# An attention-and-mixer kernel on one core: in what order a unit's products, the channel weights and GpSimd's sums are issued

## The chip, the core and the metric

The kernel runs on one core of a Trainium2 chip. A core has five engines that take their instructions in order, each from its own list: TensorE (PE in the profile, with its weight loads as PEld), VectorE (DVE), ScalarE (ACT), GpSimd (POOL) and SyncE (SP, which here only starts transfers). They wait for one another through semaphores. The metric is the device time of one execution in microseconds (us).

## The reference

Eight batches, eight heads of 64, sequence 576. First comes linear attention, then a mixer block of two small networks, one over the sequence and one over the channels:

```
q_s = softmax(q, over the head's 64);  k_s = softmax(k, over the 576 rows)
x   = q_s @ (k_s^T @ v)                         # per batch and head; heads side by side: x is 8 x 576 x 512
h   = relu(x^T @ w_tok1) @ w_tok2               # 576 -> 256 -> 576
u   = x + h^T
out = u + relu(u @ w_ch1) @ w_ch2               # 512 -> 1536 -> 512
```

The five activations are float32. The weights arrive as float64 and are turned into float32 in the kernel.

## The kernel before

**Work.** A unit is a batch b and a pair of heads j, 32 in all (n = 4b + j). The first eight (`NE`) are the early units, handled before the channel network begins; the others run between its steps. A group g is 512 columns of u, nine in all. A step (g, f) is one of twelve 128-wide slices of the 1536 channels: `ch1` forms 12 matmuls (L377) into a PSUM bank, ScalarE writes `h2h` = relu (L379) and VectorE the remainder `h2l` (L380); `ch2` forms 12 more (L388) into four accumulators `ps_o`. Every product of the channel network is done three times, high with high, high with low and low with high part, so weights and u exist as pairs (c1h/c1l, c2h/c2l, uh/ul). Emptying means taking a result out of PSUM: L379/L380 for a step, L365/L366 for a unit's u.

**A unit's stages.** `soft(n)` is both softmaxes (`softmax_k`: maximum L205, exponential L209, transposes L212 and L215 for an early unit; `softmax_q`: L233 to L239). `pe_stages(n)` gives four functions: the first transposes q and forms kv (`stage_qT` L282, for late units VectorE's transpose L294 and the copies L302; `stage_kv` L256, the reciprocal L262 and ScalarE's scaled copy `kvf`, L266), the second y (`stage_y`, L316, copied out in L318), the third h1 (`stage_h1`, L324, emptied in L331/L332) and the first half of u, the fourth the second half (`stage_u`, L359).

**Weights.** A piece is 128 x 512 float64 (512 KB). It is brought into a staging tile `stg` (L154, SyncE) and narrowed: VectorE L162, ScalarE L163, VectorE L164, L165, L167, L169. `split` (L102/L103) then makes the high part on ScalarE and the low one on VectorE. `load_tok1` brings w_tok1 in two pieces and a tail of half the width, `split_tok1` splits it for the late units, `load_tok2` brings w_tok2, and `load_ch(f)` two pieces, one of w_ch1 and one of w_ch2.

**Order.** The steps run (0, 0..3), (1, 0..11), (0, 4..11), then the groups 2 to 8. Early units are issued one after another, with unit n+2's loads and softmax ahead of unit n's h1 and u; `load_ch(0)` and `load_ch(1)` stand behind units 5 and 6, `load_ch(2)` to `load_ch(11)` before the steps 0 to 9. At the end of a group `residual` (GpSimd) forms uh + ul into a staging tile (L402). Group 0 is interrupted after four steps; its four accumulators are copied to `part` (L409), and after its last step GpSimd adds uh (L395) and ul (L396) to `part`. `out_end` adds the accumulators (L411, VectorE) and sends the result (L412, ScalarE's queue).

The text's order is a priority, not the final list: a scheduling pass places each instruction on its engine by readiness in a model of the time, earlier ones first. So an instruction that stands late in the text may run early, as L395 does. The list is fixed before the run.

```
        if n + 2 < NE:
            begin(n + 2)
            soft(n + 2)
        st[2]()
        st[3]()
```

Of the kernel before, what the change touches and what calls it, by code (L numbers as in the profile page):

```python
# [1 line left out]

# [6 lines left out]
F32 = mybir.dt.float32  # L9
F32R = mybir.dt.float32r  # L10
U32 = mybir.dt.uint32
AF = mybir.ActivationFunctionType
ALU = mybir.AluOpType
# [7 lines left out]
def attn_mixer_kernel(ctx: ExitStack, tc: tile.TileContext, q, k, kt, v, wt, out, dims):  # L21
# [15 lines left out]
    F_HEAD, F_MORE = 4, 8  # L37

    const = ctx.enter_context(tc.tile_pool(name="const", bufs=1))
    sm = ctx.enter_context(tc.tile_pool(name="sm", bufs=2))  # L40
    stg = ctx.enter_context(tc.tile_pool(name="stg", bufs=2))
    cv = ctx.enter_context(tc.tile_pool(name="cv", bufs=2))
# [24 lines left out]
    def kv_tile(pool, i):  # L67

        t = pool.tile([P, P], F32, name=f"kvf{i}")
        nc.gpsimd.memset(t, 0.0)  # L70
        return t
# [25 lines left out]
    def f32(ap):  # L97
        return ap.bitcast(F32)
# [87 lines left out]
    def split_tok1():  # L186
        split(w1h, w1l, w1f[:, 0:C, :], nc.vector)
        split(w1th, w1tl, w1t, nc.vector)
# [148 lines left out]
    uT = [slots[i] for i in (0, 1, 2, 1, 0, 2, 1, 0, 2)]  # L337
    assert len(uT) == NG

    def stage_u(u, half):  # L340
        b, j = u["b"], u["j"]
        edge = (b + 1) * CW - b * S
        cut = min(max(edge, S - 320), 320)
        n0, n1 = ((0, cut), (cut, S))[half]
        N = n1 - n0
        ns = slice(n0, n1)
        t = ps_unit()
        if u["early"]:
            mm = [(u["kvf"], u["qt"][:, ns])]
        else:  # L350
            mm = [(u["kvh"], u["qth"][:, ns]), (u["kvh"], u["qtl"][:, ns]), (u["kvl"], u["qth"][:, ns])]
        for n in range(NT):
            mm += [
                (u["hh"][:, n, :], w2h[:, n, ns]),
                (u["hh"][:, n, :], w2l[:, n, ns]),
                (u["hl"][:, n, :], w2h[:, n, ns]),
            ]
        for i, (a, w) in enumerate(mm):
            nc.tensor.matmul(t[:, 0:N], a, w, start=(i == 0), stop=(i == len(mm) - 1))  # L359
        for g, a0, a1 in ((b, n0, min(n1, edge)), (b + 1, max(n0, edge), n1)):  # L360
            if a0 < a1:
                at = b * S + a0 - g * CW
                uh, ul = (x[:, j, at : at + a1 - a0] for x in uT[g])
                src = t[:, a0 - n0 : a1 - n0]
                nc.scalar.copy(uh, src)  # L365
                nc.vector.tensor_tensor(ul, src, f32(uh), op=ALU.subtract)  # L366


    def ch1(g, f):
        hh = hpool.tile([P, CW], F32R, name="h2h")  # L370
        hl = hpool.tile([P, CW], F32R, name="h2l")
        t = ps_h.tile([P, 512], F32, name="ps_h")
        i = 0
        for n in range(NJ):
            uh, ul = (x[:, n, :] for x in uT[g])
            for a, w in ((c1h, uh), (c1l, uh), (c1h, ul)):
                nc.tensor.matmul(t, a[:, f, n, :], w, start=(i == 0), stop=(i == 3 * NJ - 1))  # L377
                i += 1
        nc.scalar.activation(hh, t, AF.Relu)  # L379
        nc.vector.scalar_tensor_tensor(hl, t, 0.0, f32(hh), op0=ALU.max, op1=ALU.subtract)  # L380
        return hh, hl

    def ch2(acc, f, first, last, hh, hl):
# [6 lines left out]
    def residual(g, n):  # L390

        uh, ul = (x[:, n, :] for x in uT[g])
        if g == 0:
            t = part[:, n, :]
            nc.gpsimd.tensor_tensor(t, t, f32(uh), op=ALU.add)  # L395
            nc.gpsimd.tensor_tensor(t, t, f32(ul), op=ALU.add)  # L396
            res[n] = t
            return
        if n % 2 == 0:
            t = stg.tile([P, CW, 2], U32, name="stg").rearrange("p n w -> p (n w)").bitcast(F32)  # L400
            res[n], res[n + 1] = t[:, 0:CW], t[:, CW : 2 * CW]
        nc.gpsimd.tensor_tensor(res[n], f32(uh), f32(ul), op=ALU.add)  # L402

    res = {}

    def out_end(g, acc, whole):
        for n, o in enumerate(acc):
# [9 lines left out]
    def begin(n):  # L417
        if n < NU and n not in units:
            units[n] = load_unit(n // NJ, n % NJ)

    def soft(n):
        if n < NU:
            softmax_k(units[n])
            softmax_q(units[n])
# [26 lines left out]
    w1t = early1.tile([P, TOK], F32, name="w1t")  # L451
    v_ring.append(v_tile(early1))
    kv_ring += [kv_tile(early1, i) for i in range(1, NB)]
    begin(0)
    load_v(0)
    soft(0)
    load_tok1()
    begin(1)
    load_v(1)
    soft(1)  # L460
    for n in range(NE):
        st = pe_stages(n)
        st[0]()
        st[1]()
        if n == 0:
            load_tok2()
        if n + 2 < NE:
            begin(n + 2)
            soft(n + 2)
        st[2]()  # L470
        st[3]()
        if n == NE - 4:
            split_tok1()
        if NE - 3 <= n < NE - 1:
            load_ch(n - (NE - 3))
    early_pools.close()
    del v_ring[1:], kv_ring[1:]
    ld = ctx.enter_context(tc.tile_pool(name="ld", bufs=2))
# [35 lines left out]
            put(x, fn)  # L514

    pend = None
    to_load = 2
    for i, (g, f) in enumerate(steps):
        if to_load < NF and (i < F_HEAD or g == 1):
            if to_load == F_MORE:  # L520
                more_pools.close()
                conv[:] = [(stg, cv)]
                c2_rows(F_MORE, NF)
            load_ch(to_load)
            to_load += 1
        h = ch1(g, f)
        for fn in todo.pop(i, []):
            fn()
# [73 lines left out]
```

## Time and profile before

| | |
|---|---|
| runs shown | 850.38, 851.43, 853.24 us; median 851.43 |
| the profiled execution | 851.01 us, its span (first to last instruction) 849.2 us |
| TensorE | 807.7 us busy (95%), 4464 matmuls, mean granted clock 0.995 |
| VectorE | 495.6 us (58%) |
| ScalarE | 323.8 us (38%) |
| GpSimd | 132.5 us (16%) |
| transfers | 63.54 MB, mean 75 GB/s |

How to read it: a line names engine, source line, operation, output tile <- input tiles and shape. In a group's line the numbers after the bar are busy time, mean ns of one, and the engine's idle time just before, with what ended it (`<-ACT h2h L379` is ScalarE's instruction of line 379 that writes h2h). A line of the timeline begins with start and duration in us; [1.42 <-DVE ...] is the idle time before it and its releaser. A line of waits gives total us, number of waits, longest. A busy TensorE is not TensorE at its peak, since matmuls are pipelined.

### The profile page before, as it was taken

Reading aid. Unit: us, or ns where it says so; the run is one execution under the profiler, and the core shown is the slowest. Engines: PE = TensorE matmul, PEld = TensorE weight load, DVE = VectorE, ACT = ScalarE, POOL = GpSimd, SP = SyncE. Lnnn points to the kernel's source line nnn. Section 1 sums busy time; section 2 is a strip of 40 time slices with the busy share of each in tenths; the row PEclk is TensorE's granted clock in tenths of the full one; section 3 lists DMA queues with packets and bytes.
Section 4 is the critical chain, followed back from the end, with each engine's and each line's share of the span. In section 5 each row is a group of like instructions: output and inputs, shape, how many; then the busy total and the mean of one; then the engine's idle time right before and its main releaser. Section 6 shows DMA issues by size and latency. Waiting matters only on the chain.

```text
span 849.2 us, 11727 instructions
## 1 busy us (share of the span) xinstructions
PE 807.7 (95%) x4464; PEld 671.8 (79%) x4464; DVE 495.6 (58%) x1076; ACT 323.8 (38%) x749; POOL 132.5 (16%) x104
## 2 busy tenths in 40 slices
PE   3779997998999999999999999999999999999997
PEld 2567885877888888888888888888888888888885
DVE  7899899988665555565557555755566322112111
ACT  4576552444553444344434344444344321011110
POOL 0000015042221111131113011311131102001000
PEclk9999999999999999999999999999999999999999
DMA  8543742223223222322213122312131001001001
GB/s 264 171 137 93 237 136 81 93 76 110 62 77 95 61 61 61 110 61 61 61 40 97 51 60 61 98 58 61 46 95 46 15 1 50 1 0 50 1 1 50
DMA packets 60632, 63.54 MB, mean 75 GB/s; under 512 B 40864, under 2 KB 40992, under 8 KB 60576
## 3 DMA queue, kind: packets, MB, share of 16 engines
q1 hardware_dynamic: 55392, 53.36, 21.5%
q10 hardware_dynamic: 5184, 9.44, 3.0%
q8 instruction: 35, 0.57, 0.3%
q14 instruction: 21, 0.17, 0.1%
HBM read 53.35 MB, written 9.44 MB: 74 GB/s over the span
## 4 chain that ended last, share of the span: by engine, by line
PE 76%; DVE 14%; DMA 5%; issue 2%; ACT 1%; POOL 1%; DVEq 0%; SPq 0%; POOLq 0%
PE ps_h L377 29%; PE ps_o L388 29%; PE ps_h L359 7%; PE ps_h L316 5%; PE ps_h L256 2%; DMA stg<-in_w 2%; DMA q_t<-in_q 2%; DVE q_t L302 2%; DVE stg L167 2%; DVE cv_s L169 1%; PE ps_h L324 1%; DVE cv_s L164 1%; DMA out<-stg 1%; PE ps_h L222 1%; DVE stg L165 1%
## 5 line engine op out<-in xcount | busy, mean ns | idle before, releaser
L380 DVE SCALAR_TENSOR_TENSOR h2l<-ps_h,h2h 128x512 fp32r<-128x512 f32 x108 | 74.0, 686 | 177.0 <-ACT h2h L379 177.0
L388 PE MATMUL ps_o<-h2h,c2h 128*128 128x512 f32 x432 | 169.9, 396 | 4.4 <-ACT h2h L379 4.4
L377 PE MATMUL ps_h<-uh,c1h 128*128 128x512 f32 x432 | 171.3, 396 | 0.0
L377 PE MATMUL ps_h<-ul,c1h 128*128 128x512 f32 x432 | 170.9, 396 | 0.0
L377 PE MATMUL ps_h<-uh,c1l 128*128 128x512 f32 x432 | 170.4, 394 | 0.0
L388 PE MATMUL ps_o<-h2h,c2l 128*128 128x512 f32 x432 | 169.8, 393 | 0.0
L379 ACT ACTIVATE h2h<-ps_h 128x512 fp32r<-128x512 f32 x108 | 64.3, 596 | 248.3 <-PE ps_h L377 240.7
L388 PE MATMUL ps_o<-h2l,c2h 128*128 128x512 f32 x432 | 154.6, 396 | 2.3 <-DVE h2l L380 2.3
L302 DVE COPY q_t<-cv_s 32x160 f32<-32x160 f32 (+1 forms) x264 | 72.8, 276 | 63.5 <-POOL ql L103 60.2
L388 PEld LDWEIGHTS ps_o<-h2h,c2h 128*128 128x128 f32 x432 | 81.7, 189 | 22.2 <-ACT h2h L379 5.3
L377 PEld LDWEIGHTS ps_h<-ul,c1h 128*128 128x128 f32 x432 | 81.3, 188 | 19.3
L388 PEld LDWEIGHTS ps_o<-h2l,c2h 128*128 128x128 f32 x432 | 79.6, 188 | 19.9 <-DVE h2l L380 3.6
L388 PEld LDWEIGHTS ps_o<-h2h,c2l 128*128 128x128 f32 x432 | 81.7, 189 | 16.8
L377 PEld LDWEIGHTS ps_h<-uh,c1h 128*128 128x128 f32 x432 | 81.3, 188 | 17.1
L377 PEld LDWEIGHTS ps_h<-uh,c1l 128*128 128x128 f32 x432 | 81.5, 189 | 16.8
L225 POOL TENSOR_TENSOR k_t<-k_t,mb 128x640 f32<-128x640 f32 x24 | 37.8, 1574 | 280.4 <-ACT mb L224 280.3
L402 POOL TENSOR_TENSOR stg<-uh,ul 128x512 f32<-128x512 f32 x32 | 41.6, 1324 | 155.8 <-DMA out<-stg 76.8
L103 POOL TENSOR_TENSOR ql<-q_t,qh 128x640 fp32r<-128x640 f32 x24 | 37.9, 1580 | 96.6 <-ACT qh L102 59.7
L233 DVE TENSOR_REDUCE st<-q_t 128x10 f32<-128x640 f32 x32 | 26.2, 818 | 42.5 <-DMA q_t<-in_q 42.5
L235 ACT ACTIVATE q_t<-q_t 128x640 f32<-128x640 f32 x32 | 23.6, 739 | 49.0 <-DVE q_t L234 49.0
L302 ACT COPY q_t<-cv_s 32x128 f32<-32x128 f32 (+1 forms) x120 | 36.8, 307 | 1.5
L359 PE MATMUL ps_h<-w2h,hh 128*128 128x256 f32 (+1 forms) x112 | 33.1, 303 | 1.4 <-ACT hh L331 1.4
(140 smaller groups left out, 1162.1 us busy)
## 6 DMA issues: line engine op xcount, KB each, us to landing
stg<-in_w SPq DMA_DIRECT2D x28, 512.0 KB, 3.7
kt_t<-in_kt SPq DMA_DIRECT2D x32, 320.0 KB, 3.5
q_t<-in_q SPq DMA_DIRECT2D x32, 320.0 KB, 3.0
v_t<-in_v SPq DMA_DIRECT2D x64, 128.0 KB, 3.0
out<-stg ACTq DMA_DIRECT2D x32, 256.0 KB, 2.7
k_t<-in_k SPq DMA_DIRECT2D x24, 320.0 KB, 3.6
v_t<-in_v SPq DMA_DIRECT2D x32, 32.0 KB, 3.1
out<-part ACTq DMA_DIRECT2D x4, 256.0 KB, 4.6
```

Of the source, the lines that this page charges most:

```text
L103: lo_eng.tensor_tensor(lo, src, f32(hi), op=ALU.subtract)
L225: nc.gpsimd.tensor_tensor(kx, kx, mb.unsqueeze(1).broadcast_to([P, C1, P]), op=ALU.subtract)
L233: nc.vector.tensor_reduce(st[:, 0, :], qt, axis=AX.X, op=ALU.max)
L235: nc.scalar.activation(qc, qc, AF.Exp)
L302: eng(qx[ys, 0:n, xs], turned[xs, 0:n, ys])
L316: nc.tensor.matmul(y[:, 0:TOK], a, w, start=(i == 0), stop=(i == len(mm) - 1))
L359: nc.tensor.matmul(t[:, 0:N], a, w, start=(i == 0), stop=(i == len(mm) - 1))
L377: nc.tensor.matmul(t, a[:, f, n, :], w, start=(i == 0), stop=(i == 3 * NJ - 1))
L379: nc.scalar.activation(hh, t, AF.Relu)
L380: nc.vector.scalar_tensor_tensor(hl, t, 0.0, f32(hh), op0=ALU.max, op1=ALU.subtract)
L388: nc.tensor.matmul(o, a[:, cs], w, start=(first and i == 0), stop=(last and i == 2))
L402: nc.gpsimd.tensor_tensor(res[n], f32(uh), f32(ul), op=ALU.add)
```

## The change

- An exponential on a one-column tile is issued first of all on ScalarE, after GpSimd has set the tile to zero.
- `load_tok1` stands ahead of unit 0's v, and unit 1's v and w_tok2 behind unit 1's softmax.
- Unit n+1's transposes, kv and y are issued ahead of unit n's h1 and u.
- `split_tok1` and the loads of f = 0 and 1 are wrapped in `behind(emptied)`, those from step 1 on in `behind(drained)`: each instruction that the block issues on ScalarE (on VectorE) is placed after the last emptying instruction on that engine. This orders instructions of one engine and adds no semaphore; the block's transfers, on SyncE, are not held.
- The loads stand before the steps 0, 1, 2, 3, 4, 6, 7, 9, 10, 12, where they stood before 0 to 9.
- Group 0's sums L395/L396 are placed behind the last residual of group 1 (L402).

```diff
     const = ctx.enter_context(tc.tile_pool(name="const", bufs=1))
+    warm = const.tile([P, 1], F32, name="warm")
+    nc.gpsimd.memset(warm, 0.0)
+    nc.scalar.activation(warm, warm, AF.Exp)
...
                 src = t[:, a0 - n0 : a1 - n0]
-                nc.scalar.copy(uh, src)
-                nc.vector.tensor_tensor(ul, src, f32(uh), op=ALU.subtract)
+                emptied[:] = [
+                    nc.scalar.copy(uh, src).ins,
+                    nc.vector.tensor_tensor(ul, src, f32(uh), op=ALU.subtract).ins,
+                ]
+    drained = []
+
+    @contextmanager
+    def behind(instructions):
+        with ExitStack() as stack:
+            for ins in instructions:
+                stack.enter_context(tc.issue_after(ins))
+            yield
...
-        nc.scalar.activation(hh, t, AF.Relu)
-        nc.vector.scalar_tensor_tensor(hl, t, 0.0, f32(hh), op0=ALU.max, op1=ALU.subtract)
+        drained[:] = [
+            nc.scalar.activation(hh, t, AF.Relu).ins,
+            nc.vector.scalar_tensor_tensor(hl, t, 0.0, f32(hh), op0=ALU.max, op1=ALU.subtract).ins,
+        ]
...
         if g == 0:
             t = part[:, n, :]
-            nc.gpsimd.tensor_tensor(t, t, f32(uh), op=ALU.add)
-            nc.gpsimd.tensor_tensor(t, t, f32(ul), op=ALU.add)
+            with behind(joined):
+                nc.gpsimd.tensor_tensor(t, t, f32(uh), op=ALU.add)
+                nc.gpsimd.tensor_tensor(t, t, f32(ul), op=ALU.add)
...
-        nc.gpsimd.tensor_tensor(res[n], f32(uh), f32(ul), op=ALU.add)
+        joined[:] = [nc.gpsimd.tensor_tensor(res[n], f32(uh), f32(ul), op=ALU.add).ins]
...
+    stages = [pe_stages(n) for n in range(NE)]
     begin(0)
-    load_v(0)
     soft(0)
     load_tok1()
+    load_v(0)
     begin(1)
+    stages[0][0]()
+    soft(1)
+    stages[0][1]()
     load_v(1)
-    soft(1)
+    load_tok2()
     for n in range(NE):
-        st = pe_stages(n)
-        st[0]()
-        st[1]()
-        if n == 0:
-            load_tok2()
         if n + 2 < NE:
             begin(n + 2)
             soft(n + 2)
-        st[2]()
-        st[3]()
-        if n == NE - 4:
-            split_tok1()
-        if NE - 3 <= n < NE - 1:
-            load_ch(n - (NE - 3))
+        if n + 1 < NE:
+            stages[n + 1][0]()
+            stages[n + 1][1]()
+        stages[n][2]()
+        stages[n][3]()
+        with behind(emptied):
+            if n == NE - 4:
+                split_tok1()
+            if NE - 3 <= n < NE - 1:
+                load_ch(n - (NE - 3))
...
-    to_load = 2
+
+    load_at = dict(zip((0, 1, 2, 3, 4, 6, 7, 9, 10, 12), range(2, NF)))
     for i, (g, f) in enumerate(steps):
-        if to_load < NF and (i < F_HEAD or g == 1):
-            if to_load == F_MORE:
+        if i in load_at:
+            if load_at[i] == F_MORE:
...
-            load_ch(to_load)
-            to_load += 1
+            with behind(drained):
+                load_ch(load_at[i])
         h = ch1(g, f)
```

More of the change, by code (lines that the diff above doesn't have):

```diff
@@ L1 @@
-from contextlib import ExitStack
+from contextlib import ExitStack, contextmanager
 import concourse.bass as bass
@@ L338, in attn_mixer_kernel @@
     assert len(uT) == NG
+    emptied = []
     def stage_u(u, half):
@@ L401, in residual @@
             res[n], res[n + 1] = t[:, 0:CW], t[:, CW : 2 * CW]
-        nc.gpsimd.tensor_tensor(res[n], f32(uh), f32(ul), op=ALU.add)
-    res = {}
+        joined[:] = [nc.gpsimd.tensor_tensor(res[n], f32(uh), f32(ul), op=ALU.add).ins]
+    res, joined = {}, []
     def out_end(g, acc, whole):
```

## The prediction

> **What bounds the kernel now.** I read the totals first, then the engines' busy times by stage, then who waits for whom on TensorE, then the order of time around its gaps.
>
> ```profile
> span 849.2 us, 11727 instructions
> PE 807.7 (95%) x4464; PEld 671.8 (79%) x4464; DVE 495.6 (58%) x1076; ACT 323.8 (38%) x749; POOL 132.5 (16%) x104
> ```
>
> ```profile
> 0.00:30.00 30.00, 13.17 (x80) 10.14 (x80) 24.71 (x56) 16.20 (x29) 2.12 (x16) 0.94 0.69 208
> 30.00:80.00 50.00, 41.68 (x317) 35.41 (x318) 44.87 (x110) 31.94 (x82) 0.00 (x0) 1.00 0.50 146
> 80.00:131.00 51.00, 51.00 (x259) 42.51 (x258) 48.41 (x91) 25.13 (x50) 7.43 (x5) 1.00 0.50 166
> 131.00:145.00 14.00, 8.75 (x32) 6.43 (x31) 14.00 (x18) 3.78 (x7) 7.70 (x5) 0.88 0.32 112
> 145.00:180.00 35.00, 35.00 (x171) 28.45 (x170) 33.95 (x56) 16.70 (x32) 7.96 (x6) 1.00 0.26 79
> 180.00:200.00 20.00, 15.89 (x78) 12.36 (x78) 16.17 (x40) 7.01 (x18) 2.90 (x2) 1.00 0.24 82
> 200.00:843.30 643.30, 642.21 (x3536) 536.49 (x3534) 311.67 (x710) 223.01 (x534) 104.38 (x72) 1.00 0.18 54
> ```
>
> The second fence's columns: stretch, its length, then the busy us (and number of instructions) of TensorE, weight load, VectorE, ScalarE, GpSimd, the granted clock, the transfers. TensorE is busy 807.7 of 849.2 us. The 41.5 idle us lie, window less busy: 16.8 before 30 us, 8.3 from 30 to 80, none to 131, 5.2 from 131 to 145, none to 180, 4.1 from 180 to 200, 1.1 to 843.3, and the last 5.9, in which only the output leaves. From 200 us on the matmuls run without a gap; the change keeps their number, so whatever it brings is TensorE idle time taken away, or added, before 200 us. No gain can pass the 34.5 us that are idle there, and the first gap is mostly waiting for the first data. The table's VectorE column is the second half of the picture: 24.7 of 30, 44.9 of 50, 48.4 of 51, 14 of 14, 34 of 35. In the head VectorE is nearly full, and its order decides who gets served.
>
> **The gaps of 30 to 80 us.** TensorE's waits in this window, all of them:
>
> ```profile
> PE ps_o L324 <- ACT kvf L266: 2.6, 2, 1.5
> PE ps_h L324 <- ACT kvf L266: 1.8, 2, 1.7
> PE ps_o L359 <- ACT hh L331: 1.7, 1, 1.7
> PE ps_o L324 <- ACT ys L318: 1.6, 1, 1.6
> PE ps_o L316 <- ACT qt L286: 0.8, 1, 0.8
> PE ps_h L256 <- DVE ul L366: 0.8, 1, 0.8
> ```
>
> They are a unit's chain: kv products, VectorE's reciprocal, ScalarE's scaled copy kvf, then h1 (L324). TensorE finds no product of the next unit in between.
>
> **The gap of 131 to 145 us.** In order of time, GpSimd's sums, VectorE beside them, TensorE and ScalarE behind:
>
> ```profile
> 123.57 5.23 POOL L395 TENSOR_TENSOR part<-part,uh 128x512 f32<-128x512 f32 x3 [120.72 <-ACT part L409]
> 133.57 5.13 POOL L396 TENSOR_TENSOR part<-part,ul 128x512 f32<-128x512 f32 x3
> ...
> 127.57 1.78 DVE L167 SCALAR_TENSOR_TENSOR stg<-stg 128x512 f32<-128x512 uint32 x1
> 129.27 3.21 DVE L165 TENSOR_SCALAR stg<-stg 128x512 uint32<-128x512 uint32 x2
> 132.41 0.68 DVE L380 SCALAR_TENSOR_TENSOR h2l<-ps_h,h2h 128x512 fp32r<-128x512 f32 x1
> ...
> 133.14 1.19 PE L388 MATMUL ps_o<-h2l,c2h 128*128 128x512 f32 x4 [1.42 <-DVE h2l L380]
> 140.94 0.80 PE L388 MATMUL ps_o<-h2h,c2h 128*128 128x512 f32 x1 [3.83 <-ACT h2h L379]
> ...
> 139.68 0.72 ACT L163 ACTIVATE cv_s<-cv_s,ebias 128x512 uint32<-128x512 uint32 x1 [4.49 <-DVE cv_s L162]
> ...
> 124.00:139.20 15.20, 15.20 (x12) 1.00 0.20 69
> ```
>
> The last line is VectorE alone in that stretch: full, with twelve instructions. While GpSimd adds, L167 takes 1.78 us and L165 1.6 each. The stretch up to 89.1 us gives the price without a sum:
>
> ```profile
> L167 DVE SCALAR_TENSOR_TENSOR stg<-stg 128x512 f32<-128x512 uint32 (+2 forms) x13 | 8.2, 627 | 0.0
> L164 DVE SCALAR_TENSOR_TENSOR cv_s<-stg,cv_s 128x512 uint32<-128x512 uint32 (+2 forms) x13 | 8.1, 626 | 0.0
> L169 DVE TENSOR_TENSOR cv_s<-stg,cv_s 128x512 f32<-128x512 f32 (+1 forms) x10 | 6.4, 637 | 0.0
> L162 DVE TENSOR_SCALAR cv_s<-stg 128x512 uint32<-128x512 uint32 (+2 forms) x14 | 5.5, 395 | 0.7 <-DMA stg<-in_w 0.7
> L165 DVE TENSOR_SCALAR stg<-stg 128x512 uint32<-128x512 uint32 (+2 forms) x13 | 5.1, 395 | 0.1
> L103 DVE TENSOR_TENSOR c1l<-cv_s,c1h 128x512 fp32r<-128x512 f32 x4 | 2.7, 679 | 0.0
> ```
>
> So VectorE loses 1.1 us on an L167 and 1.2 on an L165. Twelve instructions of 0.4 to 0.7 us are some 6 to 7 us of work, and they filled 15.2: about 9 us are lost. h2l (L380), which reads PSUM, is not longer (0.68). It comes late because it queues, and h2h because ScalarE sits before a weight piece's L163 that waits for VectorE's L162. TensorE loses 5.2 us, and 8.75 busy us at a granted clock of 0.88 cost 1.0 more: 6.3.
>
> **The change part by part.**
>
> ```profile
> 3.96 1.28 ACT L209 ACT_TABLE_LOAD   x1 [3.96 <-DMA kt_t<-in_kt]
> 20.23 1.21 DVE L103 TENSOR_TENSOR w1l<-w1f,w1h 128x1024 fp32r<-128x1024 f32 x1
> 27.16 0.42 DVE L169 TENSOR_TENSOR w1t<-stg,cv_s 128x256 f32<-128x256 f32 x1
> 28.30 0.60 PE L316 MATMUL ps_h<-w1f,q_t 128*128 128x256 f32 x2
> ```
>
> Early table load and a one-column memset: the load's 1.28 us move to before the first data. Unit 0's exponential follows it at once, but VectorE, which works on unit 0's q meanwhile, does not wait for it: I take 0, between 1.28 won and, were GpSimd's start late by the memset, the same lost.
>
> w_tok1 ahead of v on SP's queue, and its split late: the three transfers of unit 0's v are issued behind the three of w_tok1, and hidden as long as kv, which comes after the k softmax, is not early. Unit 0's y ends at 28.3 because the tail of w_tok1 is ready only at 27.2, with the split's w1l (1.21 us) ahead of it on VectorE. The split now stands behind unit 4's emptying, at the same price, where two channel pieces less stand. Gain 1.2 if only w1l leaves, 3 if y's whole wait moves up; loss 1 if v comes late. I take 1, nearest the lower bound, because the next limit is w_tok2, whose order to the units' softmax stays.
>
> A unit's first products ahead of the last unit's end: transposes, kv and y of unit n+1 now stand before h1 and u of unit n, so that the chain above has matmuls to hide behind: y alone is ten L316 of 0.3 us, by the row of two. What softmax and transposes of a unit ahead issue (SP's loads of kt and q too) keeps its place before them. The idle time is 8.3; between 0 and 8.3 I take 4.3, about what the two rows of kvf hold (4.4): the other four wait for ScalarE or VectorE themselves, which stay as full.
>
> ```profile
> 176.57 2.99 POOL L402 TENSOR_TENSOR stg<-uh,ul 128x512 f32<-128x512 f32 x2 [1.23 <-DVE cv_s L169]
> 178.33 5.08 DVE L302 COPY q_t<-cv_s 32x160 f32<-32x160 f32 x11
> 193.05 2.73 DVE L302 COPY q_t<-cv_s 32x160 f32<-32x160 f32 x11
> ```
>
> GpSimd's sums behind g=1's residuals (L402): 6.3 are won at 131 to 145. The eight sums run then after 176 us, where the last residuals of g=1 stand, into a stretch with VectorE busy 16.2 of 20. They are needed only at step 24, eight steps on, so GpSimd's own lateness costs nothing, but a late unit's softmax subtraction (L225) and ql can queue behind them, 1.7 us for each sum. The cost there is between 0 (they fall beside h2l alone) and the 9 that VectorE lost. I take 3: half of what it cost TensorE before, since no weight piece stands there any more.
>
> [...]
>
> Channel weights behind each step's emptying: no instruction and no semaphore is added, only order on VectorE and ScalarE; the loads on SP stay bound to their buffers, and softmax that was behind a held piece may go ahead of it. A piece costs 0.395+0.626+0.395+0.627+0.637+0.679 = 3.4 us of VectorE.
>
> ```profile
> 43.00:89.10 46.10, 39.99 (x314) 34.31 (x313) 42.71 (x106) 32.05 (x81) 0.00 (x0) 1.00 0.39 115
> 89.13 0.58 PE L377 MATMUL ps_h<-uh,c1h 128*128 128x512 f32 x1
> 174.12 1.77 DVE L103 TENSOR_TENSOR c1l<-cv_s,c1h 128x512 fp32r<-128x512 f32 x1
> ```
>
> Of the 13 L164 before 89.1 six are token weights, so seven channel pieces (23.6 us) were squeezed in between the units. Now two pieces wait for unit 5's emptying, two for unit 6's, two (step 0's load, whose list is still empty) for nothing, and the rest for steps. VectorE must still get through all of it: the last c1l ended at 175.9; less the 9 us of collision, 166.9, plus the time x that VectorE newly idles. TensorE wants it at: first product 89.1, less the 5.3 won above, 83.8; plus the old 86.9 from there to 176, less 6.3: 164.4. So it waits 2.5 + x. x is between 0 and the holes of the units' phase: 42.7 less 23.6 leaves 19.1 for units; with two to six pieces back (6.7 to 20.2) VectorE has 26 to 39 us of work beside TensorE's 40, so x is 1 to 14. I take x = 0 in the sum, near its lower end, since units that run closer together shorten the phase itself: a loss of 2.5.
>
> **Sum.** -1 - 4.3 - 6.3 + 3 + 2.5 = -6.1. The profiled execution took 851.0 (span 849.2 and 1.8 around it), 0.4 below the median of the runs, 851.43: 851.0 - 6.1 = 844.9.
>
> **Rivals.** A, both locks open: the head's chain waits vanish (-8.3), y moves up (-3), the sums cost nothing at their new place and the weights are never late: 851.0 - 8.3 - 3 - 6.3 = 833.4. For it speaks that TensorE ran 80 to 131 us with no idle while VectorE served everything; against it that VectorE has no slack until 180.
>
> C, the collision only moves: the sums block L302's copies and the late units' multiplications, and all 9 us reach TensorE, which already waits 4.1 us there: 844.9 + 6 = 850.9, no change. For it: the 5.08 beside 2.73. Against: TensorE has eight steps there that need only h2l.
>
> D, slower: the weights come too late. VectorE idles in the units' phase because pieces must stand behind emptyings, and the debt falls due at the last step of g=1. With x = 14 TensorE waits 16.5 instead of 2.5: 858.9. It decides from x = 8.7, where the time passes 851.0 + 2.6. For it: 48.4 of 51 and 34 of 35 busy us from 80 on leave nothing to catch up with. Against: step 0's unbound load, and 9 us of freed collisions.
>
> **How the numbers follow.** Forecast 0.50 (own range 838 to 849), A 0.15, C 0.15, D 0.20. About 0.3% (2.6 us) can be told from no change. The forecast gives faster but for 0.03, A faster, C 0.03 faster and the rest the same, D slower but for 0.01: faster 0.65, same 0.16, slower 0.19. The range 831 to 858 leaves out the far halves of A's and D's spread.
>
> **What would show it.** Right: L324's waits for kvf under 3 us before 80; L377's first product near 84; L395 behind L402, near 175; no gap over 2 us at 120 to 150; L165 at 0.4 there. Wrong: L377 waiting for c1h or c1l; VectorE idle between 45 and 80 by more than 8 us; L302's copies over 1 us each near 180 with h1 or u late; unit 0's kv waiting for v.

## The result: 14 us slower

The changed kernel took 865.19 us (median of five runs, 864.21 to 867.31); the kernel before took 850.38 beside it (850.14 to 853.24). The ratio is 1.0164, 95% interval [1.0143, 1.0185], that is 1.64% or 14.0 us; the two medians differ by 14.8. The prediction was 844.9, faster, and its range ended at 858.

Up to the first unit's stages the new lines are 3 further down than the old ones (L302 is now L305, L103 is L106, and what was L165 is now L168, while the new L165 is the old L162); the emptying of u is L371/L372, the first products of a step L393 (old L377), its emptying L396/L397, its second products L406 (old L388), GpSimd's sums into `part` L414/L415 (old L395/L396), its sums for the other groups L421 (old L402). First the totals of the page after:

```profile
span 865.5 us, 11729 instructions
...
PE 815.7 (94%) x4464; PEld 677.0 (78%) x4464; DVE 500.0 (58%) x1076; ACT 323.5 (37%) x750; POOL 128.6 (15%) x105
```

The span is 16.3 us longer (865.5 against 849.2; this execution, 867.31, is the longest of the five). TensorE is busy 8.0 us more with the same 4464 products, which is read below as a colder clock, about half of the loss; its idle time is 865.5 - 815.7 = 49.8 instead of 41.5, 8.3 more. The table by stage of the changed kernel, columns as in the prediction's second fence:

```profile
0.00:30.00 30.00, 14.16 (x78) 10.76 (x79) 23.40 (x52) 15.95 (x30) 2.15 (x17) 0.94 0.76 233
30.00:80.00 50.00, 50.00 (x383) 43.50 (x383) 37.34 (x97) 31.09 (x84) 0.00 (x0) 1.00 0.41 112
80.00:131.00 51.00, 37.85 (x144) 28.61 (x144) 46.01 (x89) 20.90 (x38) 1.82 (x1) 0.87 0.46 155
131.00:145.00 14.00, 14.00 (x62) 11.45 (x62) 14.00 (x27) 8.12 (x15) 0.00 (x0) 1.00 0.34 112
145.00:180.00 35.00, 35.00 (x155) 28.57 (x154) 31.64 (x56) 14.26 (x25) 3.54 (x3) 1.00 0.35 115
180.00:200.00 20.00, 9.79 (x67) 7.82 (x66) 19.83 (x22) 3.92 (x11) 15.26 (x12) 0.85 0.13 32
200.00:220.00 20.00, 18.41 (x95) 14.50 (x96) 16.05 (x35) 9.36 (x25) 3.75 (x3) 0.90 0.31 104
```

What was to go is gone: TensorE's idle 8.3 us of 30 to 80, and 5.2 of 131 to 145. What came: 13.2 us idle at 80 to 131, where there were none; 10.2 at 180 to 200, where there were 4.1; and 1.6 behind it. The clock column carries the rest: 37.85 busy us at 0.87, 9.79 at 0.85 and 18.41 at 0.90 lose 4.9 + 1.5 + 1.8 = 8.2, where the kernel before lost 1.0 at 131 to 145. Now the VectorE column: between 30 and 80 it is busy 37.3 of 50, where it was 44.9. The engine that was nearly full now stands still for 12.7 us, while TensorE does not wait at all.

TensorE's waits to 300 us in the changed kernel (total, number, longest), the four of them that stand for the two new gaps:

```profile
PE ps_o L406 <- DVE h2l L397: 11.5, 2, 10.2
PE ps_h L393 <- ACT c1h L105: 7.2, 3, 5.2
...
PE ps_o L406 <- ACT h2h L396: 3.5, 4, 1.9
...
PE ps_h L393 <- DVE c1l L106: 1.4, 1, 1.4
```

And its timeline, read from three engines: SyncE's weight transfers (start, duration), VectorE's work on the weights (L165 begins a piece, L172 is the last to read its staging tile, L106 forms its low part) and TensorE's wait for it, then GpSimd's sums with VectorE and TensorE beside them (the row of eleven copies holds six of 32x160 and five of 32x128):

```profile
35.48 0.33 SPq L157 DMA_DIRECT2D stg<-in_w  x1
41.45 0.34 SPq L157 DMA_DIRECT2D stg<-in_w  x1
81.11 0.34 SPq L157 DMA_DIRECT2D stg<-in_w  x1
...
75.44 0.75 DVE L165 TENSOR_SCALAR cv_s<-stg 128x512 uint32<-128x512 uint32 x2
80.41 1.28 DVE L172 TENSOR_TENSOR cv_s<-stg,cv_s 128x512 f32<-128x512 f32 x2
82.21 0.68 DVE L106 TENSOR_TENSOR c1l<-cv_s,c1h 128x512 fp32r<-128x512 f32 x1
98.11 0.63 DVE L106 TENSOR_TENSOR c1l<-cv_s,c1h 128x512 fp32r<-128x512 f32 x1
...
96.64 0.80 PE L393 MATMUL ps_h<-uh,c1h 128*128 128x512 f32 x1 [5.24 <-ACT c1h L105]
...
183.96 2.55 POOL L421 TENSOR_TENSOR stg<-uh,ul 128x512 f32<-128x512 f32 x2 [2.56 <-DVE cv_s L172]
186.46 5.00 POOL L414 TENSOR_TENSOR part<-part,uh 128x512 f32<-128x512 f32 x4
191.41 1.54 POOL L228 TENSOR_TENSOR k_t<-k_t,mb 128x640 f32<-128x640 f32 x1
192.89 4.93 POOL L415 TENSOR_TENSOR part<-part,ul 128x512 f32<-128x512 f32 x4
...
183.81 12.88 DVE L305 COPY q_t<-cv_s 32x160 f32<-32x160 f32 x11
199.12 0.65 DVE L397 SCALAR_TENSOR_TENSOR h2l<-ps_h,h2h 128x512 fp32r<-128x512 f32 x1
...
199.82 0.80 PE L406 MATMUL ps_o<-h2l,c2h 128*128 128x512 f32 x1 [10.21 <-DVE h2l L397]
```

By 41.45 ten weight transfers have been issued, six pieces of token weights and the four of f = 0 and f = 1, which fill the four staging tiles. The pieces of f = 0 wait for unit 5's emptying and begin at 75.44 (L165). The next transfer, the first piece of f = 2, goes out only at 81.11: until 68.96 SyncE's list holds other loads, and then it waits 12.1 us for VectorE's L172, the last reader of a held staging tile. The low part c1l of f = 0 is formed at 82.2, just in time, that of f = 1 only at 98.1, and TensorE waits. At the other gap eleven short copies take 12.88 us beside GpSimd's sums, and h2l, which TensorE needs, is behind them in VectorE's list.

### The profile page after: what moved, and what is told of

It is laid out like the page before. It is cut to its first block, busy times and chain, and to the rows that moved or that the text cites. A ratio compares the mean times of both kernels' runs of the same rounds, so it can differ in the third digit from the quotient of the medians.

```text
span 865.5 us, 11729 instructions
## 1 busy us (share of the span) xinstructions
PE 815.7 (94%) x4464; PEld 677.0 (78%) x4464; DVE 500.0 (58%) x1076; ACT 323.5 (37%) x750; POOL 128.6 (15%) x105
## 4 chain that ended last, share of the span: by engine, by line
PE 72%; DVE 16%; DMA 7%; issue 2%; ACT 1%; POOL 1%; SPq 0%; DVEq 0%; POOLq 0%; ACTq 0%
PE ps_h L393 26%; PE ps_o L406 26%; PE ps_h L364 7%; PE ps_h L319 5%; DMA stg<-in_w 4%; DVE q_t L305 3%; PE ps_h L259 2%; DMA out<-stg 2%; DVE cv_s L172 1%; DMA q_t<-in_q 1%; DVE cv_s L167 1%; PE ps_o L364 1%; PE ps_h L327 1%; DVE stg L170 1%; DVE h2l L397 1%
## 5 line engine op out<-in xcount | busy, mean ns | idle before, releaser
L393 PE MATMUL ps_h<-uh,c1h 128*128 128x512 f32 x432 | 172.8, 400 | 7.2 <-ACT c1h L105 7.2
L397 DVE SCALAR_TENSOR_TENSOR h2l<-ps_h,h2h 128x512 fp32r<-128x512 f32 x108 | 74.1, 687 | 176.7 <-ACT h2h L396 176.4
L406 PE MATMUL ps_o<-h2h,c2h 128*128 128x512 f32 x432 | 171.6, 398 | 3.5 <-ACT h2h L396 3.5
L393 PE MATMUL ps_h<-uh,c1l 128*128 128x512 f32 x432 | 171.7, 398 | 1.4 <-DVE c1l L106 1.4
L393 PE MATMUL ps_h<-ul,c1h 128*128 128x512 f32 x432 | 171.8, 398 | 0.0
L406 PE MATMUL ps_o<-h2h,c2l 128*128 128x512 f32 x432 | 170.7, 395 | 0.0
L406 PE MATMUL ps_o<-h2l,c2h 128*128 128x512 f32 x432 | 155.4, 399 | 11.5 <-DVE h2l L397 11.5
L396 ACT ACTIVATE h2h<-ps_h 128x512 fp32r<-128x512 f32 x108 | 64.2, 595 | 241.0 <-PE ps_h L393 236.0
L305 DVE COPY q_t<-cv_s 32x160 f32<-32x160 f32 (+1 forms) x264 | 80.6, 305 | 64.0 <-POOL ql L106 60.8
L406 PEld LDWEIGHTS ps_o<-h2l,c2h 128*128 128x128 f32 x432 | 80.4, 190 | 29.0 <-DVE h2l L397 12.4
L393 PEld LDWEIGHTS ps_h<-uh,c1h 128*128 128x128 f32 x432 | 82.1, 190 | 25.6 <-ACT c1h L105 8.4
L406 PEld LDWEIGHTS ps_o<-h2h,c2h 128*128 128x128 f32 x432 | 82.1, 190 | 22.0 <-ACT h2h L396 4.9
L393 PEld LDWEIGHTS ps_h<-uh,c1l 128*128 128x128 f32 x432 | 82.2, 190 | 19.1 <-DVE c1l L106 2.0
L393 PEld LDWEIGHTS ps_h<-ul,c1h 128*128 128x128 f32 x432 | 82.0, 190 | 19.4
L406 PEld LDWEIGHTS ps_o<-h2h,c2l 128*128 128x128 f32 x432 | 82.0, 190 | 16.9
L228 POOL TENSOR_TENSOR k_t<-k_t,mb 128x640 f32<-128x640 f32 x24 | 38.0, 1582 | 321.6 <-ACT mb L227 321.6
L106 POOL TENSOR_TENSOR ql<-q_t,qh 128x640 fp32r<-128x640 f32 x24 | 37.8, 1576 | 194.2 <-ACT qh L105 158.7
L421 POOL TENSOR_TENSOR stg<-uh,ul 128x512 f32<-128x512 f32 x32 | 41.2, 1308 | 158.3 <-DMA out<-stg 82.7
L305 ACT COPY q_t<-cv_s 32x128 f32<-32x128 f32 (+1 forms) x120 | 36.8, 307 | 6.1 <-DVE cv_s L297 4.5
```

The costliest lines, as they stand in the source:

```text
L106: lo_eng.tensor_tensor(lo, src, f32(hi), op=ALU.subtract)
L228: nc.gpsimd.tensor_tensor(kx, kx, mb.unsqueeze(1).broadcast_to([P, C1, P]), op=ALU.subtract)
L305: eng(qx[ys, 0:n, xs], turned[xs, 0:n, ys])
L396: nc.scalar.activation(hh, t, AF.Relu).ins,
L406: nc.tensor.matmul(o, a[:, cs], w, start=(first and i == 0), stop=(last and i == 2))
L421: joined[:] = [nc.gpsimd.tensor_tensor(res[n], f32(uh), f32(ul), op=ALU.add).ins]
```

## The experiments

All in one table. Each ratio is against the kernel before in the same set of runs. "None held" is the changed kernel without the holds on channel weights.

| | us | ratio to before, 95% |
|---|---|---|
| changed kernel | 865.19 | 1.0164 [1.0143, 1.0185] |
| none held (`a_nohold`) | 841.18 | 0.9868 [0.9836, 0.9901] |
| units' pairs held, steps' free (`a_holdunits`) | 857.02 | 1.0042 [1.0023, 1.0061] |
| steps' held, units' pairs free (`a_holdsteps`) | 848.61 | 0.9951 [0.9934, 0.9968] |
| only f = 0 held (`n_hold0`) | 858.27 | 1.0066 [1.0040, 1.0092] |
| only f = 1 held (`n_hold1`) | 859.28 | 1.0077 [1.0053, 1.0101] |
| f = 0 held, more scratch (`n_hold0scr`) | 859.44 | 1.0091 [1.0074, 1.0108] |
| none held, units in the old order (`n_oldunits`) | 851.87 | 0.9980 [0.9959, 1.0002] |
| none held, old start (`n_oldstart`) | 853.03 | 0.9998 [0.9985, 1.0012] |
| none held, w_tok1's split free (`n_splitfree`) | 842.62 | 0.9883 [0.9847, 0.9918] |
| none held, old steps of the loads (`n_oldload`) | 841.15 | 0.9863 [0.9840, 0.9886] |
| before with the units' new order (`b_units`) | 850.86 | 0.9969 [0.9948, 0.9991] |
| changed, units in the old order (`a_oldunits`) | 860.44 | 1.0118 [1.0088, 1.0147] |
| before with late sums (`b_sumslate`) | 853.73 | 1.0022 [1.0002, 1.0042] |
| changed with free sums (`a_sumsfree`) | 869.59 | 1.0199 [1.0173, 1.0225] |
| before without sums (`b_nosums`) | 844.28 | 0.9897 [0.9867, 0.9927] |
| changed without sums (`a_nosums`) | 861.14 | 1.0092 [1.0066, 1.0119] |
| none held, without sums (`n_nosums`) | 839.79 | 0.9832 [0.9799, 0.9865] |
| none held, sums on TensorE (`n_sumspe`) | 837.46 | 0.9811 [0.9786, 0.9836] |

### The holds on channel weights

First everything that is held on `load_ch` was let go; w_tok1's split stays held.

```
-            with behind(drained):
-                load_ch(load_at[i])
+            load_ch(load_at[i])
...
-            if NE - 3 <= n < NE - 1:
-                load_ch(n - (NE - 3))
+        if NE - 3 <= n < NE - 1:
+            load_ch(n - (NE - 3))
```

> The changed kernel with the loads of channel weights no longer ordered behind emptyings (w_tok1's split still is, and the spread-out places of the loads stay). Theory W, the held weights starve TensorE: the 13.2 us idle between 80 and 131 us fall under 3, with most of the cold clock there (about 5 us at 0.87), the gap at 180 to 200 stays near 10: about 850 us, 15 less than the changed kernel. Rival V, VectorE has simply too much work before the last weight: the idle time only moves to 30 to 80 us or to 140 to 180, and the time stays within 3 us of 865.

It took 841.18: the loss turned into a gain, and the holds cost 1.0164 - 0.9868 = 2.96%, 25 us. Its table by stage, and SyncE's transfers:

```profile
30.00:80.00 50.00, 49.63 (x386) 43.52 (x385) 48.19 (x122) 36.21 (x93) 0.00 (x0) 1.00 0.53 142
80.00:131.00 51.00, 51.00 (x230) 41.87 (x229) 48.90 (x95) 25.18 (x46) 2.19 (x1) 1.00 0.51 167
...
180.00:200.00 20.00, 16.73 (x95) 13.60 (x95) 17.54 (x31) 7.95 (x22) 12.01 (x9) 0.91 0.36 109
...
49.70 0.34 SPq L157 DMA_DIRECT2D stg<-in_w  x1
67.43 15.51 SPq L157 DMA_DIRECT2D stg<-in_w  x5
```

VectorE is full again between 30 and 80 (48.2), transfers go out at 49.7 and from 67.4 on, and the gap of 80 to 131 is gone. Then each half of the holds by itself:

```
 a_holdunits:  of the diff above, only load_ch(load_at[i]) is let go
 a_holdsteps:  only load_ch(n - (NE - 3)) is let go
```

> The changed kernel with only the two channel pairs behind units 5's and 6's emptyings held; the pieces loaded in the steps are free. What is open: which of the two holds costs the 24 us between the changed kernel (865) and the one without either (841). Theory Wu (the held pieces of the units' phase sit in the four staging tiles, so that the next transfer cannot be issued before they go, and VectorE stands idle 12.7 us between 30 and 80): this kernel is as slow as the changed one, 858 to 868, with TensorE waiting for c1h or c1l near 96 and VectorE busy 36 to 39 in 30 to 80. Rival Ws (the holds behind the steps keep the late pieces back): most of the 24 us are won here, 840 to 848, VectorE busy over 44 in 30 to 80, no gap at 80 to 131.

> The mirror: the changed kernel with only the pieces loaded in the steps held behind each step's emptying; the pairs of units 5 and 6 are free. Theory Wu: nearly all is won, 840 to 848, TensorE idle under 2 us in 30 to 131, VectorE busy over 44 in 30 to 80. Rival Ws: 855 to 866, with TensorE waiting for c1h or c1l in the steps.

Both halves cost. The units' pairs cost 2.13% (18 us) with the steps' held and 1.74% (15 us) with them free; the steps' cost 1.22% (10 us) and 0.83% (7 us). The first theory holds for the larger part, its rival for the smaller; both times lie about 1 us outside the ranges that the first theory had given. The kernel with the units' pairs held, then the one with the steps' held:

```profile
30.00:80.00 50.00, 49.50 (x383) 43.07 (x382) 37.76 (x99) 31.09 (x84) 0.00 (x0) 1.00 0.39 107
80.00:131.00 51.00, 37.00 (x137) 27.43 (x136) 47.27 (x90) 21.77 (x39) 1.80 (x1) 0.83 0.50 165
```

```profile
30.00:80.00 50.00, 48.99 (x382) 42.91 (x381) 48.12 (x120) 35.28 (x92) 0.00 (x0) 1.00 0.50 142
80.00:131.00 51.00, 45.95 (x200) 37.27 (x199) 46.42 (x89) 23.58 (x43) 1.68 (x1) 0.93 0.48 155
```

It is the units' holds that empty VectorE's list between 30 and 80; 14 idle us of TensorE follow behind 80. With the steps' held alone VectorE stays full, and 5 us follow. Which piece of the units' phase does it?

```
-        if NE - 3 <= n < NE - 1:
-            load_ch(n - (NE - 3))
+            if n == NE - 3:              # behind(emptied); n_hold1: n == NE - 2
+                load_ch(0)               #                  n_hold1: load_ch(1)
+        if n == NE - 2:                  # free;            n_hold1: n == NE - 3
+            load_ch(1)                   #                  n_hold1: load_ch(0)
```

> The version without holds on channel weights (841.2), with only the pair of f = 0 held behind unit 5's emptying; the pair of f = 1 and all the rest are free. With both pairs held it took 857.0. Theory R (the held pieces sit in the rings of staging and scratch tiles, whose later users wait: it is the first held piece that stops VectorE's supply, and f = 1 and f = 2 queue behind it): most of the 16 us are here, 850 to 857, VectorE busy 37 to 43 in 30 to 80. Rival E (what costs is the late piece itself, f = 1, which TensorE waited 5.2 us for at 96): 841 to 846, VectorE busy over 45.

> The mirror: only the pair of f = 1 held, behind unit 6's emptying; f = 0 is free. Theory R: f = 0 passes through and only the supply behind f = 1 stops, for less time: 843 to 850, VectorE busy 42 to 46 in 30 to 80. Rival E: 850 to 857, with TensorE waiting some 5 us for c1h of f = 1 near 96.

Each pair alone costs 17 us (1.98% and 2.09% above none held), as much as both. So neither theory was right: not the first held piece alone, and not one late piece. Either hold is enough. VectorE was busy 37.8 of 50 in the one and 38.6 in the other, and f = 1 was late in both, also where it was not held itself. In the kernel with f = 0 alone held, the c1l of f = 0 and f = 1:

```profile
81.87 0.68 DVE L106 TENSOR_TENSOR c1l<-cv_s,c1h 128x512 fp32r<-128x512 f32 x1
...
98.09 0.63 DVE L106 TENSOR_TENSOR c1l<-cv_s,c1h 128x512 fp32r<-128x512 f32 x1
```

How does the hold reach f = 1 where f = 1 is free? It uses the two scratch tiles that f = 0 uses, and two more were added:

```
+    cv_early = early_pools.enter_context(tc.tile_pool(name="cv_early", bufs=2))
-    conv[:] = [(stg, cv), (stg_more, cv)]
+    conv[:] = [(stg, cv), (stg_more, cv_early)]
```

> The version with only f = 0's pair held (858.3), with two scratch tiles more in the units' phase, so that the free pair of f = 1 no longer waits for the scratch tiles of the held one; the staging tiles stay four. Theory R (the rings pass a hold on to the pieces behind it): f = 1's c1l, at 98.1 in the version with two scratch tiles, comes before 92, TensorE's wait of 5.6 us for c1h near 96 is gone, 848 to 854. Rival Q (the order of VectorE's list alone, in which a late piece stands behind the late units' softmax, whatever tiles are free): 856 to 860, c1l of f = 1 still after 95.

```profile
87.75 0.68 DVE L106 TENSOR_TENSOR c1l<-cv_s,c1h 128x512 fp32r<-128x512 f32 x1
...
93.80 0.68 DVE L106 TENSOR_TENSOR c1l<-cv_s,c1h 128x512 fp32r<-128x512 f32 x1
```

f = 1 came 4 us earlier, not the 6 that were expected, and f = 0 came later. The time was no better (859.44, in the range of rival Q, whose date for f = 1 it missed): VectorE was busy 34.3 us between 30 and 80, and the next weight transfer after that of 32.2 went out at 85.7. So the scratch tiles alone are not the way. VectorE's timeline of this kernel (L373 is the emptying of u, L166 the first instruction of a piece) shows what is:

```profile
78.17 0.29 DVE L373 TENSOR_TENSOR ul<-ps_h,uh 128x128 fp32r<-128x128 f32 x1 [0.26 <-ACT uh L372]
78.38 1.43 DVE L166 TENSOR_SCALAR cv_s<-stg 128x512 uint32<-128x512 uint32 x4
```

The four are the pieces of f = 0 and f = 1. Those of f = 1 are not held, had been issued to their staging tiles by 33.8 and had scratch tiles of their own; still they run in one row with the held ones. What kept them is their place in VectorE's list, which is fixed before the run. The transfers behind them wait for the staging tiles: 12.1 us of queue time in the changed kernel, 13.8 here. In every kernel with a held pair VectorE idles 11 to 16 us between 30 and 80, in those of the new order without one 1.2 to 1.9.

### The unit order, the start and the split

```
 b_units: before, with the loop of the change
     for n in range(NE):
         begin(n + 2); soft(n + 2)
+        stages[n + 1][0](); stages[n + 1][1]()
         stages[n][2](); stages[n][3]()
```

> The kernel before with one part of the change: a unit's transposes, kv and y ahead of the last unit's h1 and u; weights, sums and start as before. Theory U, the order of products alone fills TensorE's gaps: idle in 30 to 80 us falls from 8.3 to under 3, about 844 us. Rival V, VectorE is full there, so that the gaps only come back elsewhere before 200 us: 849 to 852.

It took 850.86, 0.3% [0.1%, 0.5%] below before, and TensorE's idle time in 30 to 80 was 8.5 as ever. Its longest wait there, of the list of waits, then TensorE and VectorE on the timeline:

```profile
PE ps_o L282 <- issue: 7.4, 1, 7.4
...
48.90 1.09 PE L282 MATMUL ps_o<-ident,q_t 128*128 128x128 f32 x4 [7.35 <-issue]
...
48.03 0.78 DVE L239 TENSOR_TENSOR q_t<-q_t,st 128x640 f32<-128x640 f32 x1
```

The waits for kvf are gone, and one wait of the same size has come: the transposes of the next q now stand ahead in TensorE's list, and that q's last softmax step (L239) ends on VectorE at 48.8. The profile names no releaser for this wait; the step that ends 0.1 us ahead is read as its cause. With none held, the unit order and the start were put back one at a time, and the split was freed:

```
 n_oldunits:  none held, loop of before (stages 0 to 3 of unit n in one turn); with it
              load_v(1) ahead of soft(1) again, stages[0][0:2] behind it
 n_oldstart:  none held, load_v(0), load_v(1) and soft(1) ahead again, stages[0][0:2] behind them
 n_splitfree: none held, split_tok1() not held either
```

> The version without the holds on channel weights (841.2), with the units' loop in the order of before: a unit's first products stand behind the last unit's end again; the start order, w_tok1's late split and the sums' new place stay. What is open: the unit order alone on the kernel before moved nothing (850.9, TensorE idle 8.5 in 30 to 80), yet the version without holds has 0.4 there. Theory H (the order of units needs the earlier start: only with both are there ready products to hide behind): the idle time of 30 to 80 comes back to 6 to 9 us, total 847 to 850. Rival H2 (the gap closes because loads and VectorE are earlier by the start order, whatever the units' order): under 2 us idle there, total 840 to 843.

> The version without holds (841.2), with the start in the order of before (v of units 0 and 1 ahead, unit 0's transposes and y behind unit 1's softmax); units' order, late split and the sums' place stay. The unit order was worth 10.7 us on this version and 1.5 to 3 on the kernel before. Theory H (it needs the earlier start: with the old one a transposed q put ahead waits for VectorE): 847 to 851, with TensorE idle 4 to 8 us in 30 to 80. Rival K (it needs w_tok1's late split or the sums' place, not the start): 841 to 844, under 2 us idle there.

> The version without the holds on channel weights (841.2), and w_tok1's split also bound to nothing, so that VectorE may take it as soon as w_tok1 is loaded, as before. Theory L (the late split is what starts the units early: 1.3 to 1.8 us of VectorE in the first 30 us, and less before each unit's q): TensorE's idle time before 30 us rises by 1 to 1.5 from 15.6, 842 to 844. Rival L2 (the split fits into a hole of VectorE's in the head): within 0.8 us of 841.2.

With none held, `n_oldunits` costs 1.1% (9.5 us) and `n_oldstart` 1.3% (11 us), both more than theory H had; the unit order alone, on the kernel before, had won 0.3%. TensorE's idle time in 30 to 80 is 8.5 with the new unit order alone, 6.9 in `n_oldstart`, 7.7 in `n_oldunits` and 0.4 with both. So the first products of a unit hide the chain of the last one only if the unit ahead has been made ready earlier: with the old start the same wait as above came back (4.3 us at 47). The converse is not shown. `n_oldunits` takes back a part of the start too (unit 0's first products stand behind unit 1's softmax in it and in `n_oldstart`), and no kernel has the whole new start with the old order. Nor is all of the 11 us the start's: in `n_oldstart` a late unit's eleven copies fell beside the sums (12.87 us at 170.8), and TensorE waited 10.5 us for h2l behind them. The late split's share is 0.15%, inside the interval.

> The version without holds (841.2), with the channel weights of f = 2 to 11 loaded in steps 0 to 9, one in each, as before, where the change spreads the last five over steps 6, 7, 9, 10 and 12. Nobody's theory gave this part a price: if it only shifts what VectorE does in its full stretch, 840 to 843; if the spread is what keeps weight pieces out of the way of the late units, 844 to 848.

(`load_at` is again 0 to 9.) 841.15, as with the new steps: this part moves nothing. Last, the old unit order in the changed kernel itself, with its holds:

> The changed kernel (865.2) with the units' loop in the order of before; the holds and the rest stay. The unit order was worth 10.7 us where nothing was held. Theory H (it closes the gaps of 30 to 80, and what is won there is lost again where TensorE waits for held weights): 864 to 868, with 6 to 9 us idle in 30 to 80 and less idle time in 80 to 131. Rival G (its worth adds up with that of the holds): 873 to 877.

860.44, ratio 1.0118 [1.0088, 1.0147]: here the new unit order does not win 9.5 us, it costs some 4. TensorE's gaps of 30 to 80 were back (5.4 us); the gap behind 80 was 11.7 instead of 13.2, that of 180 to 200 was 2.2 instead of 10.2, and that of 200 to 220 4.4 instead of 1.6. What TensorE saves by running the units closer together it loses again, 1.5 us of it behind 80 and more at 180 to 220, where in the changed kernel the eleven copies fall beside the sums (12.88 us) and here they do not (1.28 + 2.70 us, at 185 to 190, ahead of the sums). So the holds have no single price: with the old unit order they cost 1.0118 - 0.9980 = 1.38% (12 us), with the new one 25, though VectorE idles 15.2 us in 30 to 80 here and 12.7 there.

### GpSimd's sums

Late sums in the kernel before, and free sums in the changed one:

```
 b_sumslate: before, the two sums of group 0 inside "with behind(joined):"
 a_sumsfree: the changed kernel without that line
```

> The kernel before with one part of the change: GpSimd's eight sums behind the residuals of group 1. Theory S: the 5.2 us gap at 131 to 145 goes, one of 8 to 12 us comes at 180 to 200 beside the copies: 854 to 857 us. The prediction's own step (6.3 won, 3 lost): about 847. Rival M: 850 as before.

> The changed kernel with GpSimd's eight sums no longer ordered behind the residuals of group 1. Theory S, the eleven short copies of a late unit are the worst neighbours of the sums, each losing over a microsecond: L305's first eleven fall from 12.9 us to under 6, the gap of 10.2 us at 180 to 200 to under 4, and a gap of some 5 us comes where the sums now run (after 134 us): about 858 us. Rival M, the collision costs the same wherever it falls: within 3 us of 865.

In neither do they find a free place. Late in the kernel before, the gap of 131 to 145 closed and eleven L302 took 12.94 us (0.2% slower, [0.0%, 0.4%]). Free in the changed kernel they ran at 132 to 149, the first three in 7.97 us, and TensorE waited 10.3 us for h2l in four places (0.35% above the changed kernel, with intervals that overlap). So what the sums cost was measured by leaving them out:

```
 b_nosums, a_nosums, n_nosums: without
-            nc.gpsimd.tensor_tensor(t, t, f32(uh), op=ALU.add)
-            nc.gpsimd.tensor_tensor(t, t, f32(ul), op=ALU.add)
```

> The kernel before with group 0's eight sums of GpSimd left out (uh and ul are not added to group 0's partial sums), so that only the price of the sums is seen. Theory M (the collision costs what TensorE idles beside it, and the cold clock behind it): 852.3 less 5.2 of idle time and 1.0 of clock, 845 to 847, no gap at 131 to 145. Rival P (VectorE owes the weights all the same, and TensorE only waits for them later): 849 to 852, with a new gap before 200.

> The changed kernel with the same eight sums left out. Theory M: what it loses at 180 to 200 is the collision with the copies of the q transpose (10.2 idle, and 2 to 3 of cold clock behind them): 865.2 less 10 to 12, 853 to 855. Rival P (the copies would be late without the sums too, since the whole stage starts late behind the weights): 860 to 865, with an idle time of over 6 at 180 to 200.

> The version without holds on channel weights (841.2) with the same eight sums left out. Theory M: less 3.3 and 2.4 of idle time at 145 to 200 and about 1 of clock: 834 to 837. Rival P: 839 to 842.

The eight sums cost 1.03% (8.8 us) in the kernel before, 0.72% (6.1) in the changed one and 0.36% (3.1, interval -0.1% to 0.8%) where none is held. Without them the gap of 180 to 200 in the changed kernel shrinks from 10.2 to 2.2, but 4.0 idle us come at 200 to 220: the late unit would still be late. So both theories hold in part: the changed kernel's time is rival P's, the small gap at 180 to 200 theory M's. Then the same work without GpSimd, the candidate:

```
+            joins = g == 0 and i > 0
+            for n, o in enumerate(acc if joins else []):
+                nc.tensor.matmul(o, ident, uT[0][0][:, n, :], start=True, stop=False)
+                nc.tensor.matmul(o, ident, uT[0][1][:, n, :], start=False, stop=False)
```

> The version without holds on channel weights with group 0's residual on TensorE: eight products of uh and ul with the identity open the accumulators of group 0's second part, in place of GpSimd's eight sums; all is computed. Eight products of 0.23 us are 1.9 us of TensorE. Theory M: 1.9 above the version with the sums left out, 836 to 839, faster than 841.2. Rival P (the sums' collision is no longer what binds): 841 to 844.

```profile
180.00:200.00 20.00, 18.64 (x115) 15.71 (x114) 16.49 (x43) 9.64 (x27) 4.39 (x3) 1.00 0.35 107
...
181.88 0.39 PE L561 MATMUL ps_o<-uh,ident 128*128 128x512 f32 x1
182.10 0.40 PE L562 MATMUL ps_o<-ul,ident 128*128 128x512 f32 x1
```

837.46, ratio 0.9811 [0.9786, 0.9836], the fastest of all, 1.9% (16 us) below the kernel before and 0.6% (5 us, interval 0.2% to 1.0%) below none held. Theory M had it 1.9 us above the version without the sums; the difference to that one (0.9832) is inside the intervals. The eight products follow each other at 0.23 us, GpSimd is busy 4.4 us of the stretch instead of 12, and the clock stays at 1.00.

## Why the prediction was wrong

The loss can be split into three differences of ratios: the start, the units' order and the split, with the sums out of both sides, 0.9832 - 0.9897 = -0.65% (-5.5 us); the sums' place, 0.36% - 1.03% = -0.67% (-5.7 us); the holds, +2.96% (+25 us). They add up to +1.64% by construction, since the same ratios enter twice with opposite signs, and other orders of taking the parts give other shares: the holds cost 2.60% (22 us) with the sums left out and 1.38% (12 us) with the old unit order. The prediction's terms for the same three were -5.3, -3.3 and +2.5. The first two differences are uncertain by 4 to 5 us each, the last by 3. Without the holds the prediction's other terms give -8.6 us; none held measured -11.2.

**Start and units' products ahead: -1 and -4.3.** As a sum this was near, within an uncertainty of 4 us, and by luck in part. Cut into two independent terms it was not right: the unit order needs the start, and alone it won 0.3%. In the changed kernel TensorE's idle time before 30 us fell by 1.0, as forecast, but that of 30 to 80 by all 8.3, not 4.3. The wait that comes when the unit order is changed alone (for the next q's softmax on VectorE) is in the prediction only as "the other four wait for ScalarE or VectorE themselves". The early table load, taken as 0, was not tried by itself.

**GpSimd's sums: -6.3 and +3.** The old place was worth 8.8; the new one cost 3.1 without holds and 6.1 with them. The forecast's reason, that no weight piece stands there any more, failed: the copies L305 stood there, and so did weight pieces (beside GpSimd a c1l took 1.76 us at 180.2, a c2l 1.66 at 196.7). Rival C had named them, with all 9 us reaching TensorE, which is near the 10.2 that the changed kernel shows at 199.8; leaving the sums out gave back 6.1 of them.

**The failed step: "Channel weights behind each step's emptying", 2.5 + x with x taken as 0.** Two things went wrong in it. The first is x. The argument was that step 0's load is not held and fills VectorE's holes, and that closer units shorten the phase. But four pieces ahead of it were held, as many as there are staging tiles, and no weight transfer went out from 41.5 to 81.1, the last 12.1 us of it for want of a staging tile. VectorE idled 12.7 us of the 50. The kernel before idles 5.1 there, so x is 7.5 by the prediction's own meaning; against the kernel without holds, which idles 1.8, it is 10.9. Both are inside the bounds of 1 to 14, and rival D was to decide from 8.7. The second is the formula. It settled the debt at one date, the last c1l before 176, and so gives 10.0 with an x of 7.5, 13.4 with 10.9 and 16.5 at most. The holds cost 25. The first dates are much earlier: f = 1 was due near 91 and came at 98, and all of TensorE's waits for c1h and c1l in the changed kernel (8.6 us) lie between 80 and 131; for the last piece, whose c1l ended at 182, it did not wait at all. The clock in and behind the new gaps was colder (0.87, 0.85 and 0.90 in the three stretches), and TensorE busy 8.0 us more; that stands nowhere in the formula. And the holds cost about twice as much with the new unit order as with the old, which no term foresaw. The holds of the steps, which had no price of their own, cost 7 to 10.

The copies beside the sums are not the holds' doing: with no channel weights held they took 12.94 us in the kernel before with late sums and 12.87 in `n_oldstart`.

So rival D's cause decided, held pieces for which VectorE idles and which then come too late, at 25 where it had 16.5 and at an earlier date than it had; C's came on top. The signs that the prediction had listed as wrong were all there but one: L393 waiting for c1h, VectorE idle by more than 8 us between 45 and 80 (11.9), the copies at 12.88 / 11 = 1.17 us each (with h2l late, where h1 or u was named); v was in time. Most of those listed as right came too: no wait for kvf, the first L393 at 82.7 (84 was forecast), no gap at 120 to 150, the old L165 at 0.42 there. The sums came behind the residuals, but at 186.5 and not near 175.

**The clock.** In the changed kernel the two stretches with waits of 5.2 and 10.2 us (80 to 131, 180 to 200) have mean granted clocks of 0.87 and 0.85, the three of the table without a gap 1.00. From 95 to 100, in which the wait of 5.2 us ends, the mean is 0.50, and from 199 to 204, in which that of 10.2 ends, it is 0.50 too. The products L393 from 99.4 to 101.1 took 0.63 us each, those from 101.8 on 0.39 to 0.40. The prediction priced the cold clock in the gap it removed (1.0), and not in those that it allowed for.

## What to carry to other kernels

When an engine is nearly full (here VectorE, 44.9 of 50 us in the kernel before), a hold need not delay only the piece that is held. Here it also delayed pieces that were free, through their place in the engine's list behind the held one, and later transfers, through the staging tiles that the held pieces kept (12.1 us in SyncE's queue). So before a piece is held, follow its tiles and its place in the list to the next users, and count the idle time that the full engine gets while it waits (12.7 us here): it came back later as waits, with a colder clock (0.85 to 0.90) on top. And before two reorderings are added up, ask whether one makes ready what the other puts ahead: the new unit order was worth 0.3% with the old start, and the gaps that it was to close went only with the new one.

## What the runs showed of the hardware

Eleven copies (six of 32x160, five of 32x128) took 12.88 us beside GpSimd's instructions (two L421, four L414, one L228, four L415, between 184 and 198, about 1.25 us each, L228 1.54), 12.94 in the kernel before with late sums, 12.87 in `n_oldstart`, and 2.7 alone (0.25 each). That is 1.17 us a copy, near the length of one sum; that each copy waited for about one sum is an estimate from these two lengths. The price here went by the number of VectorE's instructions, not by their length, and the prediction did not reckon with that: beside sums a copy of 0.25 us took 0.9 more, a tensor_scalar of 0.40 us (old L165) 1.2 more, and a scalar_tensor_tensor of 0.63 us (old L167, from staging tile to staging tile) 1.1 more. h2l, read from PSUM, kept its 0.68 us beside them (at 132.4 in the kernel before, at 178.7 in the changed one), and was late only by its place in the list.
